# Where the third layer's weight sums are made, and when its first inputs are loaded

## The chip, the cores and the metric

The kernel runs on one core of a Trainium2 chip. The metric is the device time of one execution in microseconds (us); 1624.13 us is the median of three runs of the kernel before. The engines are named as in the profile: PE (TensorE; PEld is its weight load), DVE (VectorE), ACT (ScalarE), POOL (GpSimd) and SP (SyncE), whose queue issues the DMAs.

## What is computed

An attention over packed queries, followed by two feed-forward blocks. Everything is float32.

```python
def sm_attn(qq, kk, vv):                       # softmax attention, scale 1/8
    ...
p_packed = sm_attn(p, k, v)                    # 8 batches, 8 heads, 32 packed rows, 64 wide
x = sm_attn(q, p_packed, p_packed)             # 576 rows a batch -> 4608 tokens, 512 wide
h = x @ w_in;  x = (h * cos(h)) @ w_out        # first and second matrix, 512 x 2048, 2048 x 512
h = x @ w_in2; out = (h * tanh(softplus(h))) @ w_out2   # third and fourth matrix
```

## The kernel before

Each float32 factor of the big products is split into a high part (a cast, `hi`) and the rest (a subtraction, `lo`), and each product is three matmuls, high by high, high by low and low by high (lines 136 to 138).

The first part of the program is a loop of 256 steps, 16 tiles of 288 tokens by 16 blocks of 128 hidden columns. A step makes h of its block (the tile `ps`, one of four PSUM banks, lines 136 to 138 with `aT` and `wab`), the chain of cosine on ACT and DVE (L740, L742, L743, L749, L750), the split of the result (`gh`: L757 on ACT, L760 on POOL), and, three steps late, 12 matmuls of the second matrix into `acc`. After 16 steps the tile of outputs goes to DRAM (`evac`, L781, L783, through the tiles `xo` to `x2d`). L750 is the last instruction that reads a step's PSUM bank. Beside the steps a table of due times (`at_pe`, `at_ew`, `at_ld`) places work of other kinds: the attention of later batches, the first matrix's weights (`w_unit`, L496, L497), and `pre2`, which converts the third and fourth matrix from their input form (L413 and L415 load `raw`, L427, L428 and L432 convert, L437 stores to `ws` in DRAM). A scheduler then orders each engine's instructions; it does not keep to the order of the steps but lets an instruction go when its tiles are free, with higher priority for the chain.

The second part multiplies with the third matrix in seven products instead of eight (a Strassen scheme): tokens in five chunks of 1024, 1024, 1024, 1024 and 512, each cut into two halves, and hidden columns in eight blocks `p` of 256. For a block, seven weight combinations `k` are needed (four sums of quarters, three plain quarters), each split into hi and lo; for a chunk, seven input combinations (`X`, also four sums and three plain quarters). `product(i, p, k)` multiplies them in 6 matmuls, the results go through adds on DVE (L946), Mish on ACT (L957, L955) and a split (L898, L899), and `l4_subs` multiplies by the fourth matrix.

In the kernel before, `w2_comb(j)` makes the seven combinations of block j during the loop of steps, at steps 180, 187 and so on up to 229: two loads from `ws` (L525), four sums on DVE (L532 to L535), casts on ACT (L548), lo halves on POOL or DVE (L550), four stores to DRAM (`wst`, L553). The tiles are of the tags `ld`, `tmp` and `raw`, and `raw` (two buffers) is shared with the loads of `pre2`. The second part then loads each combination as a tile `ws` with a DMA of 256 KB (L877), five products ahead, for all five chunks.

The inputs of the first chunk come from `x2d`: `x_load` (L798) at steps 248 and 253, then `x_sums` (L810 to L813) and `x_split` (L824 on ACT, L825 on DVE or POOL) in the steps behind. The split tiles are of the tags `wa` and `wb` (`wab_tile`), four buffers each, which until steps 223 and 255 hold the first matrix's weights of the last two batches. The fourth matrix's weights are loaded and split by `w2o_load` (L566, L570, L574) from step 243 on.

Of the kernel before, what the change touches and what calls it, by code (L numbers as in the profile page):

```python
# [56 lines left out]
X2_AT = 248  # L57
COMB = (180, 7)
# [20 lines left out]
def build(tc, q, k, v, p, w1i, w1o, w2i, w2o, out):  # L79
    nc = tc.nc  # L80
    ctx = ExitStack()
    with ctx:
# [435 lines left out]
        def w2_comb(j):  # L518
            st = {}

            def load():
                st["c"] = []
                for c in range(2):
                    r = ld_tile([128, 512])
                    nc.sync.dma_start(r, w2s[("i", j, c)])  # L525
                    st["c"].append(r.rearrange("p (a f) -> p a f", f=256))

            def sums():
                c0, c1 = st["c"]
                a11, a21, a12, a22 = c0[:, :, :128], c0[:, :, 128:], c1[:, :, :128], c1[:, :, 128:]  # L530
                sa, sb = [tmp_tile([128, 2, 2, 128]) for _ in range(2)]
# [4 lines left out]
                st["b"] = ((a11, a12), (sa,), (sb,), (a22,))  # L536

            def split(k):
                def f():
                    parts = st["b"][k]  # L540
                    r = tp.tile([128, 2, 2, 2, 128], F32R, tag="raw", bufs=2, name=nm("hl"))
                    for x, src in enumerate(parts):
                        w = len(src.shape) == 4
                        for hl in range(2):
                            d = r[:, :, hl] if w else r[:, x, hl]
                            h = r[:, :, 0] if w else r[:, x, 0]
                            if hl == 0:
                                nc.scalar.copy(d, src)  # L548
                            else:
                                (nc.gpsimd if k < 2 else nc.vector).tensor_tensor(d, src, h, ALU.subtract)  # L550
# [3 lines left out]
                    for x in range(n):  # L554
                        WST[(j, ((0, 1), (5, 2), (6, 3), (4,))[k][x])] = t[:, x]
# [376 lines left out]
        for m in range(TMP_BUFS):  # L932
            ws_load(m)
# [106 lines left out]
```

## Time and profile before

| | |
|---|---|
| median of 3 runs | 1624.13 us (1622.72 to 1624.3) |
| the profiled execution's own time | 1623.2 us |
| its span, first to last instruction | 1621.4 us |
| granted clock of PE, mean | 0.983 |
| PE busy | 1533.1 us, 95% of the span |
| DVE, ACT, POOL busy | 961.3 us (59%), 813.2 (50%), 393.5 (24%) |

The loop of steps ends at about 882 us, and the second part takes the rest. The mean shares hide that the two parts differ: in the loop, DVE and ACT are busy for most of the time and PE has idle times; in the second part PE is busy throughout. So a stretch has to be read on its own, with PE's idle time and granted clock first, then who PE waits for, and then what that engine is doing.

### The profile page before, as it was taken

To read this page: it belongs to the slowest core of one execution; us is meant where nothing else is said; L and a number is where in the kernel's file an instruction comes from. 1 tells how busy PE (TensorE), PEld (TensorE's weight loads), DVE (VectorE), ACT (ScalarE), POOL (GpSimd) and SP (SyncE) were. 2 spreads that over 40 slices of the span, in tenths; PEclk is the share of its full clock that TensorE was granted. 3 is DMA by queue.
4 is the path that set the end of the run, shared out by engine and by line. 5 is a ranking of instruction groups with operands and counts; after the bars stand their busy time and mean duration, and the time that the engine had idled before them with its cause. 6 is when DMAs were issued, how large, how long until landed. Compare 5 with 4: busy or idle time off the path is not lost. (4 is left out here: it accounts for less than half of the span.)

```text
span 1621.4 us, 27105 instructions
## 1 busy us (share of the span) xinstructions
PE 1533.1 (95%) x9776; PEld 1292.4 (80%) x9776; DVE 961.3 (59%) x1894; ACT 813.2 (50%) x1640; POOL 393.5 (24%) x402
## 2 busy tenths in 40 slices
PE   3978999999999999988898999999999999999999
PEld 1557788799977998788796888888888888888898
DVE  4886667766756667787878436434643364435343
ACT  3665667665666666666665324323432343234233
POOL 0452323333323333444545002100110012001100
PEclk9789999999999999999999999999999999999999
DMA  9869685532635324655645333243424332433164
GB/s 289 280 193 219 163 217 153 132 90 66 174 88 146 90 69 151 236 175 203 219 153 168 127 124 124 75 143 121 128 72 143 124 120 67 141 122 123 53 197 135
DMA packets 143749, 235.61 MB, mean 145 GB/s; under 512 B 28928, under 2 KB 54016, under 8 KB 143616
## 3 DMA queue, kind: packets, MB, share of 16 engines
q1 hardware_dynamic: 143616, 233.89, 47.9%
q8 instruction: 77, 1.26, 0.3%
q14 instruction: 56, 0.46, 0.1%
HBM read 187.70 MB, written 46.14 MB: 144 GB/s over the span
## 5 line engine op out<-in xcount | busy, mean ns | idle before, releaser
L760 POOL TENSOR_TENSOR gh<-r,gh 128x288 fp32r<-128x288 f32 x256 | 215.5, 848 | 387.0 <-ACT gh L757 305.2
L137 PE MATMUL acc<-gh,wo 128*128 128x288 f32 x1024 | 303.7, 302 | 0.9 <-POOL gh L760 0.9
L138 PE MATMUL acc<-gh,wo 128*128 128x288 f32 x1024 | 298.3, 299 | 0.0
L136 PE MATMUL acc<-gh,wo 128*128 128x288 f32 x1024 | 284.4, 306 | 13.6 <-ACT gh L757 4.4
L136 PEld LDWEIGHTS acc<-gh,wo 128*128 128x128 f32 x1024 | 186.0, 192 | 49.7 <-issue 20.9
L137 PEld LDWEIGHTS acc<-gh,wo 128*128 128x128 f32 x1024 | 195.7, 191 | 15.2 <-issue 7.6
L138 PEld LDWEIGHTS acc<-gh,wo 128*128 128x128 f32 x1024 | 194.6, 191 | 6.6 <-issue 6.4
L136 PE MATMUL ps<-aT,wab 128*128 128x288 f32 x512 | 162.0, 316 | 21.8 <-DVE r L750 17.3
L749 ACT ACTIVATE r<-r,halfpi 128x288 f32<-128x288 f32 x256 | 136.0, 535 | 86.6 <-DVE r L743 81.9
L957 ACT ACTIVATE c<-c 128x512 f32<-128x512 f32 (+1 forms) x96 | 53.8, 561 | 242.6 <-DVE c L946 242.3
L740 ACT ACTIVATE ki<-ps,quarter 128x288 int32<-128x288 f32 x256 | 124.9, 495 | 61.6 <-PE ps L138 55.3
L137 PE MATMUL ps<-aT,wab 128*128 128x288 f32 x512 | 154.2, 301 | 0.0
L138 PE MATMUL ps<-aT,wab 128*128 128x288 f32 x512 | 153.7, 301 | 0.0
L750 DVE TENSOR_TENSOR r<-r,ps 128x288 f32<-128x288 f32 x256 | 114.6, 449 | 63.2 <-ACT r L749 62.2
L742 DVE SCALAR_TENSOR_TENSOR r<-ki,ps 128x288 f32<-128x288 int32 x256 | 114.0, 447 | 60.0 <-ACT ki L740 46.8
L136 PEld LDWEIGHTS ps<-aT,wab 128*128 128x128 f32 x512 | 98.9, 193 | 44.6 <-DVE r L750 23.7
L757 ACT CAST gh<-r 128x288 fp32r<-128x288 f32 x256 | 108.4, 429 | 50.1 <-DVE r L750 28.4
L743 DVE TENSOR_SCALAR r<-r 128x288 f32<-128x288 f32 x256 | 122.7, 482 | 3.8
L137 PE MATMUL acc<-wo,gh 128*128 128x512 f32 x320 | 125.0, 391 | 0.0
L136 PE MATMUL acc<-wo,gh 128*128 128x512 f32 x320 | 124.9, 390 | 0.0
L136 PE MATMUL ps<-wab,ws 128*128 128x512 f32 (+1 forms) x336 | 119.5, 356 | 5.1 <-DVE r L750 2.5
L138 PE MATMUL acc<-wo,gh 128*128 128x512 f32 x320 | 124.2, 389 | 0.0
(144 smaller groups left out, 3157.1 us busy)
## 6 DMA issues: line engine op xcount, KB each, us to landing
ws<-wst SPq DMA_DIRECT2D x280, 256.0 KB, 2.6
ld<-ws SPq DMA_DIRECT2D x96, 256.0 KB, 3.3
kr<-in_k_dram SPq DMA_DIRECT2D x64, 272.0 KB, 5.6
raw<-in_moe_w_out_dram SPq DMA_DIRECT2D x32, 512.0 KB, 4.4
kr<-in_q_dram SPq DMA_DIRECT2D x60, 272.0 KB, 5.5
wst<-hl SPq DMA_DIRECT2D x24, 512.0 KB, 3.1
x2d<-xo SPq DMA_DIRECT2D x64, 144.0 KB, 1.8
out_dram<-ld SPq DMA_DIRECT2D x36, 256.0 KB, 2.2
```

Source lines behind the costliest of these rows:

```text
L136: nc.tensor.matmul(ps, l0, r0, start=first, stop=False)
L137: nc.tensor.matmul(ps, l0, r1, start=False, stop=False)
L138: nc.tensor.matmul(ps, l1, r0, start=False, stop=last)
L740: nc.scalar.activation(ki, st["h"], AF.Identity, bias=quarter, scale=1.0 / TWO_PI)
L742: nc.vector.scalar_tensor_tensor(r, ki, -TWO_PI, st["h"], ALU.mult, ALU.add)
L743: (nc.gpsimd if n % C_MOD in C_POOL else nc.vector).tensor_scalar(r, r, 1.570796, -4.712388, ALU.min, ALU.max)
L749: nc.scalar.activation(g, g, AF.Sin, bias=halfpi, scale=1.0)
L750: nc.vector.tensor_tensor(g, g, st["h"], ALU.mult)
L757: nc.scalar.copy(gh[:, 0], st["g"])
L760: nc.gpsimd.tensor_tensor(gh[:, 1], st["g"], gh[:, 0], ALU.subtract)
L957: nc.scalar.activation(c, c, AF.Mish)
```

## The change

The sums and splits of the third matrix's weights leave the loop of steps, but for the first. `comb_load(0)` stands at step 240, `comb_sums(0)` at 242, the first five splits (`ws_load(0)` to `ws_load(4)`) at 243 to 247, `comb_load(1)` at 244. All others stand in the first chunk of tokens of the second part: after the first product of block p the sums of block p + 1 are made and the loads of block p + 2 issued, and after every product one more combination is split straight into the tile `ws` that a product five later uses, and stored to `wst`. The four later chunks load from `wst` as before. So for the first chunk 56 loads of 256 KB turn into 56 stores and 16 loads, and the loop of steps loses 16 loads and 32 stores less what blocks 0 and 1 need.

The inputs of the first chunk are loaded at steps 231 and 232 (into a `kr` tile, which the queries used), their sums stand at 233 and 234, four of the seven splits at 234 to 239 (into `wa`) and the other three at 247, 251 and 255 (into `wb`). One sum is now made in place. POOL makes the lo halves of the combinations with even k, DVE those with odd k; before it was the other way round. The last two also hold for the later chunks.

```diff
-X2_AT = 248
-COMB = (180, 7)
+X2_AT = 231
+COMB = 240
...
-        def w2_comb(j):
...
-                nc.vector.tensor_tensor(sa[:, 0], a21, a22, ALU.add)
-                nc.vector.tensor_tensor(sa[:, 1], sa[:, 0], a11, ALU.subtract)
-                nc.vector.tensor_tensor(sb[:, 1], a11, a21, ALU.subtract)
-                nc.vector.tensor_tensor(sb[:, 0], a12, sa[:, 1], ALU.subtract)
...
-                                (nc.gpsimd if k < 2 else nc.vector).tensor_tensor(d, src, h, ALU.subtract)
...
-                    nc.sync.dma_start(t, r[:, :n].bitcast(F32))
...
+        def comb_load(p):
+            CB[p] = []
+            for c in range(2):
+                r = ld_tile([128, 512])
+                nc.sync.dma_start(r, w2s[("i", p, c)])
+                CB[p].append(r.rearrange("p (a f) -> p a f", f=256))
+
+        def comb_sums(p):
...
+            r = tp.tile([128, 4, 2, 128], F32, tag="raw", bufs=2, name=nm("sw"))
+            nc.vector.tensor_tensor(r[:, 0], a21, a22, ALU.add)
+            nc.vector.tensor_tensor(r[:, 1], r[:, 0], a11, ALU.subtract)
+            nc.vector.tensor_tensor(r[:, 2], a11, a21, ALU.subtract)
+            nc.vector.tensor_tensor(r[:, 3], a12, r[:, 1], ALU.subtract)
+            CB[p] = (a11, a12, r[:, 1], r[:, 2], a22, r[:, 0], r[:, 3])
...
+        def ws_load(m):
...
+            w = WS[m] = tp.tile([128, 2, 2, 128], F32R, tag="tmp", bufs=TMP_BUFS, name=nm("ws"))
+            if m < 56:
+                nc.scalar.copy(w[:, 0], CB[p][k])
+                (nc.gpsimd if k % 3 == 2 else nc.vector).tensor_tensor(w[:, 1], CB[p][k], w[:, 0], ALU.subtract)
+                d = WST[(p, k)] = dram.tile([128, 2, 2, 128], F32, name=nm("wst"))
+                nc.sync.dma_start(d, w.bitcast(F32))
+            else:
+                nc.sync.dma_start(w.bitcast(F32), WST[(p, k)])
...
-        for j in range(8):
-            load, fs = w2_comb(j)
-            at_ld(COMB[0] + COMB[1] * j, load)
-            for i, f in enumerate(fs):
-                at_ew(COMB[0] + COMB[1] * j + 2 + i, f)
+        at_ld(COMB, lambda: comb_load(0))
+        at_ew(COMB + 2, lambda: comb_sums(0))
+        for m in range(TMP_BUFS):
+            at_ew(COMB + 3 + m, lambda m=m: ws_load(m))
+        at_ld(COMB + 4, lambda: comb_load(1))
...
+                if i == 0:
+                    r = kr_tile([128, 2, 1024])
+                    rs = [r[:, 0], r[:, 1]]
...
-                nc.vector.tensor_tensor(t1, b12, b11, ALU.subtract)
-                nc.vector.tensor_tensor(t2, b22, t1, ALU.subtract)
+                t2, t3, t4 = [ld_tile([128, 512])[:, :n] for _ in range(3)]
                 nc.vector.tensor_tensor(t3, b22, b12, ALU.subtract)
+                nc.vector.tensor_tensor(b12, b12, b11, ALU.subtract)
+                nc.vector.tensor_tensor(t2, b22, b12, ALU.subtract)
...
-                    X[(i, k)] = wab_tile(k // 4, [128, 2, 2, 512], F32R)
+                    X[(i, k)] = wab_tile((0, 1, 0, 0, 0, 1, 1)[k], [128, 2, 2, 512], F32R)
...
-                (nc.gpsimd if k % 2 else nc.vector).tensor_tensor(x[:, a, 1, :n], src, x[:, a, 0, :n], ALU.subtract)
+                (nc.gpsimd if k % 2 == 0 else nc.vector).tensor_tensor(x[:, a, 1, :n], src, x[:, a, 0, :n], ALU.subtract)
...
+        xu = x_units(0)
+        for a in range(2):
+            at_ld(X2_AT + a, xu[9 * a])
+            at_ew(X2_AT + 2 + a, xu[9 * a + 1])
+            for u, kk in enumerate((2, 3, 4, 0)):
+                at_ew(X2_AT + 3 + 2 * a + u, xu[9 * a + 2 + kk])
+            for u, kk in enumerate((1, 5, 6)):
+                at_ew(247 + 4 * u, xu[9 * a + 2 + kk])
...
             for a in range(2):
                 mm3(ps, w[:, 0, a], w[:, 1, a], x[:, a, 0, :n], x[:, a, 1, :n], a == 0, a == 1)
+            if i == 0 and k == 0 and p < 7:
+                comb_sums(p + 1)
+                if p < 6:
+                    comb_load(p + 2)
             ws_load(m + TMP_BUFS)
```

The change shifts the line numbers: L742, L743 and L750 of before are L734, L735 and L742 of the changed kernel, L784 is L776, L946 is L936 and L899 is L891.

DVE, among the steps at which the weights of the last pair of batches (`wab`, L497) are made. Before, the sums of the third matrix's first block (L532 to L535) stand between the chains:

```order
L532 TENSOR_TENSOR tmp_8483<-ld_8402,ld_8404 128x256
L534 TENSOR_TENSOR tmp_8484<-ld_8402 128x256
L533 TENSOR_TENSOR tmp_8483<-tmp_8483,ld_8402 128x256
L742 SCALAR_TENSOR_TENSOR r_8392<-ki_8390,ps_8369 128x288
L535 TENSOR_TENSOR tmp_8484<-ld_8404,tmp_8483 128x256
L743 TENSOR_SCALAR r_8392<-r_8392 128x288
L742 SCALAR_TENSOR_TENSOR r_8439<-ki_8437,ps_8406 128x288
L750 TENSOR_TENSOR r_8392<-r_8392,ps_8369 128x288
L743 TENSOR_SCALAR r_8439<-r_8439 128x288
L750 TENSOR_TENSOR r_8439<-r_8439,ps_8406 128x288
```

The changed kernel at the same weights, with its own line numbers (L804 and L805 are two sums of the inputs, in a `kr` tile):

```order
L734 SCALAR_TENSOR_TENSOR r_8517<-ki_8515,ps_8494 128x288
L735 TENSOR_SCALAR r_8517<-r_8517 128x288
L734 SCALAR_TENSOR_TENSOR r_8548<-ki_8546,ps_8525 128x288
L735 TENSOR_SCALAR r_8548<-r_8548 128x288
L742 TENSOR_TENSOR r_8517<-r_8517,ps_8494 128x288
L742 TENSOR_TENSOR r_8548<-r_8548,ps_8525 128x288
L734 SCALAR_TENSOR_TENSOR r_8589<-ki_8587,ps_8556 128x288
L735 TENSOR_SCALAR r_8589<-r_8589 128x288
L742 TENSOR_TENSOR r_8589<-r_8589,ps_8556 128x288
L804 TENSOR_TENSOR ld_10067<-kr_9986 128x512
L805 TENSOR_TENSOR kr_9986<-kr_9986 128x512
L734 SCALAR_TENSOR_TENSOR r_8629<-ki_8627,ps_8606 128x288
```

The four weight sums are gone from there, and the first sums of the inputs have come up from the end of the loop to this place.

SP, some forty steps on, where the fourth matrix is converted. Before (L553 stores a split of the third matrix's weights, L566 loads for the fourth matrix's splits):

```order
L553 DMA wst_9781<-hl_9778 128x1024
L437 DMA ws_9853<-tmp_9813 128x512
L553 DMA wst_9820<-hl_9817 128x512
L415 DMA raw_9822<-in_moe_w_out_dram 128x1024
L566 DMA ld_10697<-ws_9247 128x512
L415 DMA raw_9855<-in_moe_w_out_dram 128x1024
L415 DMA raw_9895<-in_moe_w_out_dram 128x1024
L437 DMA ws_9926<-tmp_9891 128x512
L437 DMA ws_9968<-tmp_9929 128x512
L566 DMA ld_10733<-ws_9295 128x512
L553 DMA wst_9980<-hl_9975 128x1024
L437 DMA ws_10011<-tmp_9971 128x512
```

The changed kernel, from the first of these raw loads on:

```order
L415 DMA raw_9053<-in_moe_w_out_dram 128x1024
L415 DMA raw_9055<-in_moe_w_out_dram 128x1024
L437 DMA ws_9086<-tmp_9049 128x512
L437 DMA ws_9124<-tmp_9089 128x512
L415 DMA raw_9093<-in_moe_w_out_dram 128x1024
L437 DMA ws_9167<-tmp_9127 128x512
L415 DMA raw_9136<-in_moe_w_out_dram 128x1024
L437 DMA ws_9169<-tmp_9132 128x512
L415 DMA raw_9176<-in_moe_w_out_dram 128x1024
L437 DMA ws_9207<-tmp_9172 128x512
L415 DMA raw_9565<-in_moe_w_out_dram 128x1024
L437 DMA ws_9248<-tmp_9210 128x512
```

The stores of hl and the loads of ld no longer stand between the raw loads and the stores of their conversions.

DVE in the third layer, from the first add of a block of weight columns on (c, u and m are the products' sums). Before:

```order
L946 TENSOR_TENSOR c_11692<-ps_11682,m_2264_11677 128x512
L946 TENSOR_TENSOR u_2271_11709<-ps_11700,m_2264_11677 128x512
L899 TENSOR_TENSOR gh_2267_11691<-c_11692,gh_2267_11691 128x512
L946 TENSOR_TENSOR u_2274_11723<-ps_11714,u_2271_11709 128x512
L946 TENSOR_TENSOR c_11738<-ps_11728,u_2274_11723 128x512
L946 TENSOR_TENSOR c_11755<-ps_11746,u_2274_11723 128x512
L946 TENSOR_TENSOR u_2271_11709<-ps_11746,u_2271_11709 128x512
L899 TENSOR_TENSOR gh_2277_11737<-c_11738,gh_2277_11737 128x512
L946 TENSOR_TENSOR c_11772<-ps_11763,u_2271_11709 128x512
```

The changed kernel, the second block (L531 to L534 are the sums of the next block, L547 a lo half):

```order
L936 TENSOR_TENSOR c_11307<-ps_11294,m_2148_11289 128x512
L547 TENSOR_TENSOR ws_11301<-sw_11131,ws_11301 128x256
L531 TENSOR_TENSOR sw_11419<-ld_11280,ld_11282 128x256
L533 TENSOR_TENSOR sw_11419<-ld_11280 128x256
L532 TENSOR_TENSOR sw_11419<-sw_11419,ld_11280 128x256
L936 TENSOR_TENSOR u_2157_11327<-ps_11315,m_2148_11289 128x512
L891 TENSOR_TENSOR gh_2152_11306<-c_11307,gh_2152_11306 128x512
L534 TENSOR_TENSOR sw_11419<-ld_11282,sw_11419 128x256
L547 TENSOR_TENSOR ws_11322<-ld_11136,ws_11322 128x256
L936 TENSOR_TENSOR u_2161_11344<-ps_11332,u_2157_11327 128x512
L547 TENSOR_TENSOR ws_11339<-ld_11138,ws_11339 128x256
L936 TENSOR_TENSOR c_11362<-ps_11349,u_2161_11344 128x512
```

Four sums and three lo halves now stand between the first five operations that this row had before; the row of a whole block has nine more.

## Rows read from the trace of the kernel before

**Rows 1.** Stretches of time: each engine's busy us and (x) instructions, granted clock, DMA share.

```profile
300.00:640.00 340.00, 335.81 (x2812) 294.34 (x2812) 230.24 (x541) 220.40 (x475) 121.99 (x139) 0.99 0.43 112
640.00:700.00 60.00, 56.35 (x432) 42.82 (x432) 46.43 (x94) 38.23 (x81) 27.11 (x28) 1.00 0.60 206
700.00:760.00 60.00, 50.05 (x346) 48.49 (x345) 47.45 (x103) 41.77 (x89) 27.19 (x29) 0.91 0.56 184
760.00:860.00 100.00, 91.42 (x668) 87.36 (x667) 79.83 (x161) 67.73 (x149) 48.88 (x52) 1.00 0.54 185
860.00:890.00 30.00, 22.10 (x112) 17.99 (x111) 24.22 (x31) 16.41 (x32) 15.43 (x12) 0.94 0.55 171
```

**Rows 2.** Waits of PE, 640 to 870 us: us in total, times, longest.

```profile
PE ps L136 <- DVE r L750: 15.6, 13, 4.2
```

**Rows 3.** DVE groups, 640 to 860 us: busy us, mean ns | idle before.

```profile
L743 DVE TENSOR_SCALAR r<-r 128x288 f32<-128x288 f32 x71 | 38.8, 547 | 0.7
...
L432 DVE SCALAR_TENSOR_TENSOR tmp<-tmp,cvt 128x512 int32<-128x512 int32 x17 | 13.2, 778 | 0.8 <-ACT tmp L427 0.3
...
L535 DVE TENSOR_TENSOR tmp<-ld,tmp 128x256 f32<-128x256 f32 x8 | 6.5, 811 | 0.0
L550 DVE TENSOR_TENSOR hl<-tmp,hl 128x512 fp32r<-128x512 f32 x8 | 5.8, 730 | 0.6 <-ACT hl L548 0.5
L534 DVE TENSOR_TENSOR tmp<-ld 128x256 f32<-128x256 f32 x8 | 5.5, 689 | 0.0
L550 DVE TENSOR_TENSOR hl<-ld,hl 128x256 fp32r<-128x256 f32 x8 | 4.5, 565 | 2.8 <-ACT hl L548 2.8
...
L532 DVE TENSOR_TENSOR tmp<-ld,ld 128x256 f32<-128x256 f32 x8 | 4.4, 546 | 0.8 <-DMA ld<-ws 0.7
```

**Rows 4.** The same view, 300 to 640 us: two groups.

```profile
L743 DVE TENSOR_SCALAR r<-r 128x288 f32<-128x288 f32 x114 | 50.6, 447 | 2.2
...
L432 DVE SCALAR_TENSOR_TENSOR tmp<-tmp,cvt 128x512 int32<-128x512 int32 x10 | 6.8, 684 | 0.0
```

**Rows 5.** Waits at the head of SP's queue, 640 to 860 us.

```profile
SPq L553 <- DVE hl L550: 27.7, 11, 4.5
SPq L553 <- POOL hl L550: 22.6, 11, 6.8
```

**Rows 6.** Groups of the whole span on POOL, DVE and ACT.

```profile
L825 DVE TENSOR_TENSOR wab<-ld,wab 128x512 fp32r<-128x512 f32 (+1 forms) x20 | 24.9, 1260 | 0.1
...
L550 POOL TENSOR_TENSOR hl<-ld,hl 128x256 fp32r<-128x256 f32 x16 | 12.2, 781 | 13.7 <-ACT hl L548 8.0 <-DMA raw<-in_moe_w_out_dram 5.7
...
L550 POOL TENSOR_TENSOR hl<-tmp,hl 128x512 fp32r<-128x512 f32 x8 | 11.2, 1404 | 4.8 <-ACT hl L548 4.6
...
L548 ACT CAST hl<-ld 128x256 fp32r<-128x256 f32 x24 | 9.2, 402 | 8.8 <-DMA wst<-hl 6.4 <-DMA ld<-ws 1.4 <-ACT gh L757 1.0
```

**Rows 7.** Stretches, as rows 1, in the third layer.

```profile
890.00:1004.00 114.00, 114.00 (x505) 94.39 (x504) 50.99 (x76) 37.83 (x62) 3.04 (x2) 1.00 0.39 127
1004.00:1046.00 42.00, 42.00 (x187) 34.77 (x186) 21.66 (x26) 15.18 (x27) 12.38 (x8) 1.00 0.24 70
```

**Rows 8.** Copies of m at L962, 870 to 1080 us: min/median/max ns, first to last start.

```profile
L962 ACT COPY m<-ps x8: 569/587/587, 883.1 to 981.4; 128x512 f32<-128x512 f32 x8
L962 ACT COPY m<-rb x3: 587/587/587, 1039.9 to 1069.8; 128x512 f32<-128x512 f32 x3
```

**Rows 9.** Three lines' instructions: min/median/max ns, first and last start.

```profile
L535 DVE TENSOR_TENSOR tmp<-ld,tmp x8: 410/630/1496, 644.3 to 796.0; 128x256 f32<-128x256 f32 x8
...
L550 DVE TENSOR_TENSOR hl<-ld,hl x8: 415/425/1014, 651.7 to 803.7; 128x256 fp32r<-128x256 f32 x8
...
L810 DVE TENSOR_TENSOR ld<-xr x10: 410/680/692, 845.6 to 1495.8; 128x512 f32<-128x512 f32 x8, 128x256 f32<-128x256 f32 x2
```

**Rows 10.** Timeline, 886 to 888 us: start, us, what [idle before].

```profile
886.10 0.46 DVE L783 COPY xo<-acc 128x288 f32<-128x288 f32 x1 [3.48 <-DMA x2d<-xo]
...
887.21 0.50 PE L136 MATMUL ps<-wab,ws 128*128 128x512 f32 x1 [1.86 <-DVE c L946]
```

More of the change, by code (lines that the diff above doesn't have):

```diff
@@ L516, in build @@
         WST = {}
-        def w2_comb(j):
[L519 to L531, printed above, removed]
-                nc.vector.tensor_tensor(sa[:, 0], a21, a22, ALU.add)
-                nc.vector.tensor_tensor(sa[:, 1], sa[:, 0], a11, ALU.subtract)
-                nc.vector.tensor_tensor(sb[:, 1], a11, a21, ALU.subtract)
-                nc.vector.tensor_tensor(sb[:, 0], a12, sa[:, 1], ALU.subtract)
[L536 to L549, printed above, removed]
-                                (nc.gpsimd if k < 2 else nc.vector).tensor_tensor(d, src, h, ALU.subtract)
-                    n = 1 if k == 3 else 2
-                    t = dram.tile([128, n, 2, 2, 128], F32, name=nm("wst"))
-                    nc.sync.dma_start(t, r[:, :n].bitcast(F32))
-                    for x in range(n):
-                        WST[(j, ((0, 1), (5, 2), (6, 3), (4,))[k][x])] = t[:, x]
-                return f
-            return load, [sums] + [split(k) for k in range(4)]
@@ new lines, in build @@
+        WS = {}
+        NQ = 56 * 5
+        def ws_load(m):
+            if m >= NQ:
+                return
+            p, k = divmod(m % 56, 7)
+            w = WS[m] = tp.tile([128, 2, 2, 128], F32R, tag="tmp", bufs=TMP_BUFS, name=nm("ws"))
[6 more added lines that the diff above has]
+                nc.sync.dma_start(w.bitcast(F32), WST[(p, k)])
@@ L791, in f @@
                 n = 1024 if i < 4 else 512
-                rs = []
-                for kc in (a, 2 + a):
-                    r = tp.tile([128, n], F32, tag="raw", bufs=2, name=nm("xr"))
+                if i == 0:
+                    r = kr_tile([128, 2, 1024])
+                    rs = [r[:, 0], r[:, 1]]
+                else:
+                    rs = [tp.tile([128, n], F32, tag="raw", bufs=2, name=nm("xr")) for _ in range(2)]
+                for r, kc in zip(rs, (a, 2 + a)):
                     lo, hi = 1024 * i, 1024 * i + n
@@ L808, in f @@
                 b11, b12, b21, b22 = b1[:, :n], b1[:, n:], b2[:, :n], b2[:, n:]
-                t1, t2, t3, t4 = [ld_tile([128, 512])[:, :n] for _ in range(4)]
-                nc.vector.tensor_tensor(t1, b12, b11, ALU.subtract)
-                nc.vector.tensor_tensor(t2, b22, t1, ALU.subtract)
+                t2, t3, t4 = [ld_tile([128, 512])[:, :n] for _ in range(3)]
                 nc.vector.tensor_tensor(t3, b22, b12, ALU.subtract)
+                nc.vector.tensor_tensor(b12, b12, b11, ALU.subtract)
+                nc.vector.tensor_tensor(t2, b22, b12, ALU.subtract)
                 nc.vector.tensor_tensor(t4, b21, t2, ALU.subtract)
-                raws[(i, a)] = (b11, b21, t2, t3, t4, t1, b22)
+                raws[(i, a)] = (b11, b21, t2, t3, t4, b12, b22)
             return f
@@ L860, in build @@
                 evac(m // NF)
-        for n in sorted(n for n in set(bg_pe) | set(bg_ew) | set(bg_ld) if n < X2_AT + 20):
+        for n in sorted(n for n in set(bg_pe) | set(bg_ew) | set(bg_ld)):
             run_bg(bg_pe, n)
@@ L930, in sub @@
                     todo.pop(0)()
-        for m in range(TMP_BUFS):
-            ws_load(m)
         for i in range(5):
```

16 lines of the change are left out of this document (3 added, 13 removed).

## The prediction

> **What bounds the kernel now.** I read first the busy time of the engines by stretch, then whom PE waited for, then the groups of DVE and the waits of SP in the stretch that stood out, and last the timeline at the change from the second matmul layer to the third.
>
> The stretches [rows 1] are to be read for two things: how long PE was idle, and whether its clock was whole. From 300 to 640 us PE is idle for 4.2 us and the granted clock is 0.99, worth 3.4 us more: 7.6 us of 340, or 2.2%. Later it is different: 3.65 us idle from 640 to 700, 9.95 from 700 to 760, 8.58 from 760 to 860, 7.90 from 860 to 890, together 30.1 us. In 700 to 760 us the granted clock is 0.91, which is 2.4 GHz with some time at 1.2 GHz in a stretch with much idle time, worth 0.09 x 60 = 5.4 us, and in 860 to 890 it is 0.94, 1.8 us. So 640 to 890 us loses 37 us; at 2.2% it would lose 5. The old sums of the third layer's weights sit just there: L535 runs from 644 to 796 us [rows 9]. After 890 us PE has no gap (114.00 of 114 us, 42.00 of 42) [rows 7]; nothing can be gained there.
>
> Whom PE waits for from 640 to 870 us: r at L750, which is DVE, 15.6 us in 13 waits [rows 2]. L750 is the last reader of the PSUM bank that holds a step's h, so DVE is late with the chain of a step and PE finds none of its four banks free. DVE is 77, 79, 80 and 81% busy in these stretches, 68% from 300 to 640 us [rows 1].
>
> **What goes from 640 to 860 us.** On DVE the old sums and lo halves are six groups: 6.5 + 5.8 + 5.5 + 4.5 + 4.4, and 4.4 again for L533, the twin of L532: 31.1 us [rows 3]. On POOL 12.2 + 11.2 = 23.4 us; on ACT 24 casts of 0.40 us and 16 of twice the width [rows 6]. On SP 16 loads and 32 stores. The stores stood at the head of SP's queue until their lo halves were made, 27.7 us for DVE and 22.6 us for POOL [rows 5], and behind them stood raw loads of the 17 conversions. In the new order of SP, raw loads and ws stores alternate with no hl store between.
>
> **What comes in.** Eight sums of the inputs and six of their lo halves (eight go to POOL) are DVE work of 0.68 to 1.26 us each [rows 9, 6], so 10 to 18 us. In the trace they begin at 846 us. In the new order the first sums stand among the very steps that lose the old ones, far ahead of step 231, since the scheduler lets work go once its tiles are free. The sums of two weight blocks and the first lo halves add some 12 operations of about 0.5 us, 6 us.
>
> **640 to 860 us, the sum.** Lost now: 22.2 idle + 5.4 clock = 27.6 us of 220, so the work itself is some 192 us. High end: if the loss of the quiet stretch goes with time, 2.2% of 192 = 4.2 us stay, a gain of 23.4. If that loss goes with its conversions, 17 against 10 [rows 3, 4], 1.7 x 7.6 = 13 us stay, a gain of 14.6. Low end: if the loss goes with DVE's work, only the net relief counts, 31.1 - 24 of 31.1, and the gain is 27.6 x 0.23 = 6.3. I take 14, near the middle of the three.
>
> **860 to 890 us.** Lost now: 7.9 + 1.8 = 9.7 us. The 1.86 us at the end [rows 10] stay: DVE's second evacuation waits 3.48 us for an xo store to land, and PE waits behind it; this isn't touched. The rest comes from the inputs' sums and lo halves and the fourth layer's weights falling together with the last steps. Most of the inputs' work has gone from here, but the new order has 91 second-layer matmuls in a row with no product between to fill a wait. Gain 0 to 7.8; I take 3.5.
>
> **The first 1024 tokens of the third layer.** A block of 256 weight columns takes 14.04 us: eight copies of m from 883.1 to 981.4 us are seven periods [rows 8]. DVE is 45% busy, 6.3 us a block; ACT 33%, 4.7 us [rows 7]. Added per block: on DVE four sums and five of seven lo halves (40 of 56), on ACT seven casts, on POOL two lo halves. A sum takes 0.41 us undisturbed, 0.81 in the mean of the dearest; a lo half 0.42 at least, 0.57 in the mean [rows 3, 9]. That is 3.7 to 6.1 us, so DVE comes to 10.0 to 12.4 of 14.04 us. ACT adds 7 x 0.40 = 2.8 and comes to 7.5. POOL gets 2 x 0.78. All fit, so PE's own 14.04 us hide the work. SP trades 56 loads of 256 KB for as many stores and 16 loads. Behind a late sum on DVE stand the adds that free PE's banks: a bank is wanted again four products later, 4 x 2.0 = 8 us after its product starts; the product takes 1.4 of them (6 matmuls of 114 / 505 = 0.226 us) and its add 0.7, so 6 us are slack. A weight tile is made five products ahead, with a similar margin. I charge 1 us for the first block, which stands without fourth-layer matmuls (42 x 0.226 = 9.5 us instead of 14); bounds 0 and 3.
>
> **Costed at nothing.** The in-place sum, three ld tiles instead of four and POOL making four of seven lo halves also hold for later tokens. The cover is the stage between the last block (981.4 + 14 us) and 1039.9 us [rows 8], 44 us in which PE works without a gap and the next inputs are split; without it one POOL lo half of 1.4 us would come late per chunk, some 6 us in four chunks.
>
> **The sum.** -14 - 3.5 + 1 = -16.5 us, against the profiled execution's own 1623.2 us (span 1621.4): 1606.7. The median of the runs is 0.9 us higher: 1607.5 us. With all ends the gain is 3 to 31 us, 1593 to 1621.
>
> **A rule weighed.** One sum took 0.41 to 1.50 us for the same shape [rows 9], and the chain's L743 took 547 ns from 640 to 860 us against 447 from 300 to 640 [rows 3, 4]. The Trainium skill, SBUF — State Buffer, section "Who interferes with whom", has a DVE tensor_tensor with two SBUF inputs contend with a GpSimd operation that reads SBUF: the second to issue blocks until the first is done; it lists tensor_scalar's faster modes as well. The trace agrees in kind: the longest sum is longer by 1.1 us, about one POOL operation. By the rule the POOL work that goes frees DVE of more than its own 31.1 us (the last rival), and the new sums in the third layer can each be blocked by a POOL lo half.
>
> **Rivals.**
> *DVE stays the bound.* 173.7 us of DVE from 640 to 860 us, less 31.1, plus 24, are 167 of some 206 us, 81%, no lighter than now. For it: the inputs land where DVE is already 77% busy. Against: the relief of SP and POOL. It gives the low end, 6.3 us, less 1: 1619 us. Chance 0.17.
> *The new work stalls the third layer; slower.* In each block four sums and lo halves stand nearly in a row on DVE between one product's add and the next. If PE waits out that row at mean prices, 0.55 + 0.69 + 0.55 + 0.81 + 2 x 0.57 = 3.7 us, eight blocks lose 30 us: 1637 us. It decides once such a row, with its wait for ACT's cast, exceeds the 6 us of slack, or once the nine added operations take more than 14.04 - 6.3 = 7.7 us a block, 0.86 us each. For it: maxima of 1.0 to 1.5 us [rows 9]. Against: POOL, next to which these maxima stood, is nearly idle in this stage (3.04 of 114 us) [rows 7]. Chance 0.09.
> *The whole hole closes.* DVE also gets back what POOL cost it, 71 x 0.10 = 7 us on L743 alone. Then 640 to 890 us runs at 2.2% and the 1.86 us: 37 - 5 - 2 = 30 us, 1594 us. Chance 0.07.
> My forecast has 0.67.
>
> **Range and chances.** A measurement of this kernel tells about 0.2%, 3.2 us, from no change. Faster: nearly all of the forecast, the last rival, more than half of the first: 0.82. Same: the rest of the first, and a stall in the third layer that eats the gain: 0.10. Slower: 0.08. The range for 8 in 10 is 1598 to 1620; it leaves out the second rival and most of the third.
>
> **What would show it.** Right: from 640 us to the first product PE loses some 13 to 20 us instead of 37, the clock is 1.00, waits for r at L750 are under 6 us, the first copy of m comes at about 866 us, and PE has no gap from then on with DVE at 70 to 88% for eight blocks. The step on the third layer is wrong if PE waits for a ws tile or for c and u in these blocks, or if a block takes over 14.3 us. The first step is wrong if L750 still leads PE's waits with more than 10 us.

## The result, and the profile of the changed kernel

The changed kernel takes 1597.52 us (median of 4 runs, 1596.92 to 1598.81) against 1623.43 us before (4 runs): a ratio of 0.9843, 95% interval 0.9826 to 0.986. The forecast was 1607.5 us, a gain of 16.5; the gain was 25.9. The time fell, as forecast, and it fell in the two places that were named; the size of one of the two was wrong, and the time lies 0.5 us below the range of 1598 to 1620.

The profiled execution took 1596.92 us (span 1595.1). Stretches, as in [rows 1] and [rows 7]; the last is the third layer's first 1024 tokens, which now begin 26 us earlier:

```profile
300.00:640.00 340.00, 334.87 (x2812) 293.67 (x2798) 227.84 (x540) 219.24 (x470) 119.95 (x136) 0.99 0.43 114
640.00:700.00 60.00, 59.60 (x464) 47.16 (x457) 40.50 (x88) 39.54 (x76) 19.61 (x21) 1.00 0.31 94
700.00:760.00 60.00, 52.34 (x376) 50.74 (x375) 51.84 (x106) 41.97 (x91) 30.54 (x30) 0.94 0.57 181
760.00:860.00 100.00, 95.16 (x694) 91.78 (x694) 76.10 (x154) 68.71 (x150) 50.97 (x51) 1.00 0.33 106
860.00:890.00 30.00, 30.00 (x134) 24.86 (x133) 20.99 (x44) 16.35 (x35) 4.45 (x5) 1.00 0.61 208
864.00:978.00 114.00, 114.00 (x504) 94.44 (x503) 67.29 (x130) 54.95 (x108) 12.58 (x15) 1.00 0.45 158
```

From 640 to 860 us PE is idle for 12.9 us, not 22.2, and from 860 to 890, where it is by now in the third layer, for none, not 7.9. What is left stands mostly from 700 to 760 us, where DVE is busier than before (51.84 against 47.45 us). All of PE's waits from 640 to 1020 us (total, times, longest), which answer to [rows 2]:

```profile
PE ps L136 <- DVE r L742: 11.7, 6, 4.7
PE acc L137 <- POOL gh L752: 0.6, 1, 0.6
PE acc L136 <- DVE xo L775: 0.4, 1, 0.4
```

Before, from 640 to 860 us, the three longest (xo is the evacuation of a tile: these waits are of the second matrix's matmuls for `acc`):

```profile
PE ps L136 <- DVE r L750: 14.5, 12, 4.2
PE acc L136 <- ACT xo L781: 3.5, 3, 2.3
PE acc L136 <- DVE xo L783: 1.6, 1, 1.6
```

So the waits for r fell by 2.8 us in this stretch, and those for xo by 4.7.

Copies of m in the third layer and the first one of the second 1024 tokens (rb), as in [rows 8], and two groups of DVE from 640 to 860 us, as in [rows 3]:

```profile
L952 ACT COPY m<-ps x8: 578/578/579, 857.5 to 955.4; 128x512 f32<-128x512 f32 x8
L952 ACT COPY m<-rb x5: 589/589/589, 1013.6 to 1073.4; 128x512 f32<-128x512 f32 x5
...
L735 DVE TENSOR_SCALAR r<-r 128x288 f32<-128x288 f32 x73 | 34.9, 481 | 1.0
...
L432 DVE SCALAR_TENSOR_TENSOR tmp<-tmp,cvt 128x512 int32<-128x512 int32 x17 | 15.5, 914 | 0.0
```

A block of weight columns takes (955.4 - 857.5) / 7 = 13.99 us, as before.

**Three marks cut the gain into parts.** ACT's first copy in the evacuation of a tile marks the tile's end; of the 16 tiles (0 to 15) I take the ends of tile 10 and tile 14. The third mark is the first rb copy. The middle part (M) from the first mark to the second is the old home of the weight sums; the end part (E) from the second to the third holds the last tile, the change of layers and all eight blocks of the first 1024 tokens, as many matmuls in every kernel here. Before, in the timeline of ACT (start, us):

```profile
630.04 0.70 ACT L781 COPY xo<-acc 128x288 f32<-128x288 f32 x2
837.16 0.69 ACT L781 COPY xo<-acc 128x288 f32<-128x288 f32 x2
```

and in the changed kernel:

```profile
627.64 0.69 ACT L773 COPY xo<-acc 128x288 f32<-128x288 f32 x2
821.36 0.39 ACT L773 COPY xo<-acc 128x288 f32<-128x288 f32 x1
```

With the rb copies at 1039.9 and 1013.6 us, M went from 207.1 to 193.7 us (13.4 less), E from 202.7 to 192.2 (10.5 less), and 2.4 us were gained ahead of 630 us, where the two programs have the same work. Together 26.3, the difference of the two profiled executions.

Between the first two marks, rounded to whole us, the engines were busy as follows, before and after:

```profile
630.00:837.00 207.00, 184.82 (x1353) 163.71 (x1350) 160.42 (x337) 136.43 (x294) 92.27 (x98) 0.98 0.58 198
```

```profile
628.00:821.00 193.00, 179.99 (x1349) 161.63 (x1342) 145.19 (x310) 127.91 (x269) 79.61 (x83) 0.98 0.37 120
```

PE's idle time went from 22.2 to 13.0 us, and the busy time of nearly the same number of matmuls from 184.8 to 180.0.

### The profile page after: what moved, and what is told of

Read it like the earlier page. It is cut to its first block, busy times and chain, and to the rows that moved or that the text cites. A ratio compares the mean times of both kernels' runs of the same rounds, so it can differ in the third digit from the quotient of the medians.

```text
span 1595.1 us, 27163 instructions
## 1 busy us (share of the span) xinstructions
PE 1523.9 (96%) x9776; PEld 1288.3 (81%) x9776; DVE 957.1 (60%) x1908; ACT 818.9 (51%) x1656; POOL 398.8 (25%) x404
## 5 line engine op out<-in xcount | busy, mean ns | idle before, releaser
L136 PE MATMUL ps<-aT,wab 128*128 128x288 f32 x512 | 160.9, 314 | 19.8 <-DVE r L742 14.6
L742 DVE TENSOR_TENSOR r<-r,ps 128x288 f32<-128x288 f32 x256 | 114.3, 449 | 63.9 <-ACT r L741 63.2
L734 DVE SCALAR_TENSOR_TENSOR r<-ki,ps 128x288 f32<-128x288 int32 x256 | 113.9, 447 | 62.7 <-ACT ki L732 50.1
L735 DVE TENSOR_SCALAR r<-r 128x288 f32<-128x288 f32 x256 | 116.4, 458 | 4.1
```

The source lines that it names most:

```text
L136: nc.tensor.matmul(ps, l0, r0, start=first, stop=False)
L734: nc.vector.scalar_tensor_tensor(r, ki, -TWO_PI, st["h"], ALU.mult, ALU.add)
L735: (nc.gpsimd if n % C_MOD in C_POOL else nc.vector).tensor_scalar(r, r, 1.570796, -4.712388, ALU.min, ALU.max)
L742: nc.vector.tensor_tensor(g, g, st["h"], ALU.mult)
```

## The experiments

Each kernel was timed in three rounds beside the kernel before. The column us is the median of the runs. M and E come from one profile each, and a profiled execution can lie off its median: that of e2 took 1618.88 us, 5.0 above, that of e1 1600.12, 3.5 below, those of e12 and e16 4.1 and 3.8 above. So differences of a few us in M are not told by these profiles alone.

| kernel | us | ratio, 95% interval | M | E |
|---|---|---|---|---|
| before | 1623.4 | 1 | 207.1 | 202.7 |
| e2, inputs alone | 1613.93 | 0.9927 to 0.9961 | 211.4 | 192.2 |
| e5, no sums | 1611.92 | 0.9908 to 0.995 | 196.2 | 202.4 |
| e6, no POOL lo halves | 1614.13 | 0.9909 to 0.996 | 195.4 | 204.1 |
| e7, no stores | 1612.99 | 0.9897 to 0.995 | 197.8 | 201.3 |
| e9, sums at 178 | 1613.83 | 0.9921 to 0.996 | 199.5 | 202.6 |
| e13, inputs at 247 | 1622.12 | 0.9971 to 1.0007 | 205.3 | 203.1 |
| e17, sums at 181 | 1620.18 | 0.996 to 0.9992 | 205.9 | 202.1 |
| e18, sums at 174 | 1620.85 | 0.9964 to 0.9993 | 205.8 | 201.9 |
| e14, conversions spread | 1619.91 | 0.9973 to 1.0 | 204.4 | 201.7 |
| e1, weights alone | 1603.66 | 0.9854 to 0.9896 | 187.9 | 201.5 |
| **changed** | 1597.52 | 0.9826 to 0.986 | 193.7 | 192.2 |
| e3, sums twice | 1596.57 | 0.981 to 0.9874 | 193.3 | 191.2 |
| e4, lo halves on POOL | 1598.14 | 0.9825 to 0.9869 | 192.8 | 191.2 |
| e8, first sums on POOL | 1599.57 | 0.9823 to 0.9866 | 192.7 | 192.2 |
| e16, weights at 238 | 1596.22 | 0.9815 to 0.986 | 192.1 | 192.4 |
| e10, inputs at 238 | 1594.67 | 0.9808 to 0.9848 | 188.0 | 193.3 |
| e12, conversions earlier | 1596.62 | 0.9816 to 0.9863 | 189.7 | 191.1 |
| e11, conversions spread | 1588.76 | 0.9765 to 0.9812 | 185.5 | 191.2 |
| e15, e10 and e11 | 1589.2 | 0.9773 to 0.9815 | 183.3 | 193.0 |

Rows down to e14 have the weight work of all eight blocks in the loop of steps, e5 to e7 less the part that is named; those from e1 on have little more there than the sums and first splits of the first two blocks.

### The two halves of the change, apart

e1 is the changed kernel with the inputs at their old steps, their splits in the old tiles and on the old engines (the load still goes to a `kr` tile, and one sum is in place); e2 is the kernel before with the inputs' part of the change alone.

```diff
-X2_AT = 231
+X2_AT = 248
...
-        xu = x_units(0)
...
+        for u, f in enumerate(x_units(0)):
```

> The weights' sums are made in the third layer as in the changed kernel, but the inputs of the first 1024 tokens stand at steps 248 and 253 as before, with the old engines and buffers for their splits (their load still goes to a kr tile and one sum is in place). Theory 1, two holes that add: the sums' removal fills 640 to 837 us (some 14 us) and the inputs' move fills the loop's end (some 10 us); this run then takes about 1609 us. Theory 2, the one on record: the inputs' move is worth 3.5 us at most; about 1601 us. Theory 3, the two need each other: 1609 us or more here, and no gain in the other run of this pair.

> The inputs are loaded and split as in the changed kernel (steps 231 and 232), while the weights' sums stay in the loop at steps 180 to 229 as before. Theory 1: about 1613 us. Theory 2: about 1620 us. Theory 3: the inputs' 10 to 18 us of DVE come into a stretch in which DVE is already late; 1622 us or more.

e1 gained 19.7 us, e2 9.4. No theory had e1's time; e2 came out by theory 1. The sum, 29.1 us, is more than the 25.9 of the whole change. The table tells where: the weights' part shortens M by 19.2 us and leaves E nearly as it was (201.5), the inputs' part shortens E by 10.5. In e2's profile M is 4.3 us longer, but not by waits:

```profile
632.00:843.00 211.00, 189.43 (x1340) 166.45 (x1333) 171.33 (x344) 140.08 (x299) 99.31 (x103) 0.94 0.60 204
```

PE's idle time is 21.6 us against 22.2 before; its busy time is 4.6 us longer, at a granted clock of 0.94 against 0.98. By the medians all of e2 but E lost only 1.1 us (10.5 - 9.4). That early inputs cost time in M is better seen between e1 and the changed kernel, where PE's waits for r in M are 5.7 and 11.7 us; M differs by 5.8, and by the medians the cost is 3.2 us (E's 9.3 less the 6.1 between the two times).

E's difference holds over all kernels: E is 201.3 to 204.1 us in the ten with late inputs and 191.1 to 193.3 in the ten with early ones, with nothing between. So the 10 us of E belong to the inputs' part, whatever else is done. This part moves the steps, the tiles of the splits and the engines of the lo halves together, and no run takes these three apart.

What stood in E is to be seen in PE's waits. Before, 837 to 890 us, the four longest:

```profile
PE ps L136 <- DVE r L750: 2.5, 2, 1.4
PE ps L137 <- DVE wab L825: 2.3, 1, 2.3
PE ps L136 <- DVE c L946: 1.9, 1, 1.9
PE ps L136 <- ACT m L962: 0.7, 1, 0.7
```

e1, 815 to 870 us, the three longest:

```profile
PE ps L136 <- DVE c L934: 2.5, 1, 2.5
PE ps L137 <- DVE wab L819: 2.3, 1, 2.3
PE ps L136 <- ACT m L950: 1.4, 1, 1.4
```

The wait of 2.3 us for wab is that of a third-layer product for its own input's lo half, which DVE had not made yet. DVE in the kernel before, at that time:

```profile
871.03 0.68 DVE L812 TENSOR_TENSOR ld<-xr,xr 128x512 f32<-128x512 f32 x1
871.63 0.44 DVE L750 TENSOR_TENSOR r<-r,ps 128x288 f32<-128x288 f32 x1
871.99 0.68 DVE L813 TENSOR_TENSOR ld<-xr,ld 128x512 f32<-128x512 f32 x1
872.60 1.78 DVE L825 TENSOR_TENSOR wab<-xr,wab 128x512 fp32r<-128x512 f32 x1
...
875.87 0.68 DVE L825 TENSOR_TENSOR wab<-ld,wab 128x512 fp32r<-128x512 f32 x1
```

The scheduler had let matmuls of the first third-layer products go ahead of the last tile's last matmuls, while their inputs were still being made; the first two of them, in PE's timeline, and the second-layer matmul behind them:

```profile
863.38 0.50 PE L136 MATMUL ps<-wab,ws 128*128 128x512 f32 x1 [1.15 <-DVE r L750]
863.72 0.40 PE L137 MATMUL ps<-wab,ws 128*128 128x512 f32 x1
863.95 0.30 PE L137 MATMUL acc<-gh,wo 128*128 128x288 f32 x1
```

L750 stood behind the sums, the product behind its lo half, and the next products behind the adds of c and u, which came after the evacuation on DVE. Which wait stands in the list differs: e13 and e18, with E as long (203.1 and 201.9 us), wait neither for wab nor for c, but for r:

```profile
PE ps L136 <- DVE r L750: 5.4, 4, 3.1
```

```profile
PE ps L136 <- DVE r L750: 5.7, 3, 4.1
```

What all ten kernels with late inputs share is that 21 to 24 product matmuls come before the last second-layer matmul; in the ten with early inputs none does. No run holds the products back while the inputs are late, so whether the early products or DVE's load at the end costs the 10 us stays open; only the inputs' part, which removes both, is shown.

In the changed kernel PE goes over without a gap (timeline of PE, start and us):

```profile
854.13 0.29 PE L138 MATMUL acc<-gh,wo 128*128 128x288 f32 x1
854.26 0.40 PE L136 MATMUL ps<-wab,ws 128*128 128x512 f32 x1
```

and the late second copy of the evacuation, with the adds of c and u behind it on DVE, is still there, but no product waits for them:

```profile
854.58 0.44 DVE L775 COPY xo<-acc 128x288 f32<-128x288 f32 x1
857.63 0.46 DVE L775 COPY xo<-acc 128x288 f32<-128x288 f32 x1 [2.61 <-ACT ws L546]
```

### Is the third layer near its limit?

e3 makes each of the sums of blocks 1 to 7 twice; e4 gives POOL all lo halves of the weights but the first five, which stay as they were.

```diff
-            nc.vector.tensor_tensor(r[:, 0], a21, a22, ALU.add)
+            for _ in range(2 if p else 1):
+                nc.vector.tensor_tensor(r[:, 0], a21, a22, ALU.add)
...
-                (nc.gpsimd if k % 3 == 2 else nc.vector).tensor_tensor(w[:, 1], CB[p][k], w[:, 0], ALU.subtract)
+                (nc.gpsimd if m >= TMP_BUFS or k % 3 == 2 else nc.vector).tensor_tensor(w[:, 1], CB[p][k], w[:, 0], ALU.subtract)
```

> The changed kernel, with the four sums of each block from the second on made twice (28 more DVE operations of 0.41 us or more, 1.6 to 2.6 us a block). If DVE has slack in the third layer, as the sum on record has it, nothing moves: 1597.5 us, blocks of 14.0 us. If the new work is close to stalling PE there, the blocks grow by up to 2.6 us, 18 us in all: 1605 to 1616 us.

> The changed kernel, with all 51 lo halves of the weights that are made in the third layer on POOL instead of 15. If POOL's reads block DVE's two-input operations as the longest rows of the kernel before suggest, 36 more POOL operations of 0.78 us cost DVE up to 28 us in the eight blocks, 3.5 us a block, and with DVE at about 11 us of 14 that is at the edge: 1597.5 to 1603 us. If PE's four banks and five weight tiles cover it: no change, 1597.5 us.

Neither moves the time. The stretch of the eight blocks, e3 first, then e4:

```profile
864.00:978.00 114.00, 114.00 (x505) 94.39 (x504) 76.99 (x153) 54.75 (x107) 13.86 (x16) 1.00 0.45 159
```

```profile
868.00:982.00 114.00, 114.00 (x505) 94.42 (x504) 58.94 (x96) 54.62 (x107) 37.87 (x48) 1.00 0.44 158
```

DVE at 68% with the sums made twice, or POOL three times as busy, leaves PE without a gap. The rival of a stalled third layer is out by a wide margin.

### What made the middle hole

e5, e6 and e7 each take one part of the old work out of the kernel before; e8 moves what is left of the sums in the loop to POOL.

```diff
-                nc.vector.tensor_tensor(sa[:, 0], a21, a22, ALU.add)
...
-                st["b"] = ((a11, a12), (sa,), (sb,), (a22,))
+                st["b"] = ((a11, a12), (a21, a22), (a12, a11), (a22,))
```

> The kernel before without the 32 DVE sums of the third layer's weights (L532 to L535, 20.8 us of DVE from 640 to 860 us in rows 3); quarters of the weights stand in their place, so the third layer multiplies by other numbers; casts, lo halves, loads and stores stay. Moving the weight sums alone gained 19.7 us (1603.7). Theory A, DVE's own busy time made the hole: 20.8 of 31.1 us of DVE go, so some 13 us of the 19.7: 1610 us, and e6 and e7 little. Theory B, the queues and POOL made it (SP's head waited 50.3 us for lo halves; a POOL operation holds DVE up): 3 to 5 us, 1618 to 1620 us.

```diff
+                        if k < 2:
+                            nc.scalar.copy(r[:, :, 0] if w else r[:, x, 0], src)
+                            continue
```

> The kernel before without POOL's 24 lo halves of the third layer's weights (L550 on POOL, 23.4 us of POOL); the hi half is stored once and loaded in both places. DVE's lo halves, the sums and the casts stay; the stores of these parts carry half the bytes and no longer wait for POOL (22.6 us at the head of SP's queue in rows 5). Theory A (DVE's own time): 1621 to 1623 us. Theory B (POOL's operations hold DVE up, and the stores that wait for them hold SP up): 8 to 12 us less, 1611 to 1615 us.

```diff
-                    nc.sync.dma_start(t, r[:, :n].bitcast(F32))
+                    if j == 0:
...
+                        nc.sync.dma_start(t, r[:, :n].bitcast(F32))
```

> The kernel before without 28 of the 32 stores of the third layer's weights (L553), those of blocks 1 to 7; the third layer reads block 0's weights in their place. All sums, casts and lo halves stay; gone are 7 MB of DMA and the waits of SP's queue for lo halves (50.3 us in rows 5), behind which the raw loads of the conversions stood. Theory A (DVE's own time): 1621 to 1623 us. Theory B (SP's queue): about 10 us less, 1611 to 1615 us.

```diff
+            eng = nc.gpsimd if p < 2 else nc.vector
+            eng.tensor_tensor(r[:, 0], a21, a22, ALU.add)
```

> The changed kernel with the eight sums of the first two blocks on POOL instead of DVE; they run at 794 to 805 us, where PE still waits 4.1 us for r. Theory A (DVE's own time is what PE waits for): DVE is freed of 5.6 us there and 2 to 3 of the 4.1 us go, 1594 to 1596 us. Theory B (a POOL operation holds DVE up for as long): no gain or a loss, 1597 to 1600 us.

The three gained 11.5, 9.3 and 10.5 us, 31 in sum, where the whole move gained 19.7. e5 came out near theory A (1610), e6 and e7 by theory B (1611 to 1615), so neither holds alone, and the parts don't add. e8 gave no gain that can be told (its interval overlaps the changed kernel's). e9 then put a question to these numbers: the same work, two steps earlier.

```diff
-COMB = (180, 7)
+COMB = (178, 7)
```

> The kernel before with the weight sums at steps 178, 185 and so on instead of 180, 187: the same work in nearly the same place. It asks how much a mere reshuffle of the order moves the time, since leaving out the sums, POOL's lo halves or the stores each gained 9 to 12 us. If those gains come from the work that was left out: within 3 us of the kernel before, 1620 to 1626 us. If the order of the kernel before is only an unlucky one: about 1612 us.

It gained 10.4 us against the kernel before of its own set (1624.25), without leaving anything out. The due times move the work by more than they say: the first block's sums begin at 619.6 us instead of 639.8, ahead of the first mark, and the last block's last sum at 775.7 instead of 796.0. Three more neighbours of the kernel before follow, e13 with `X2_AT = 247`, e17 with `COMB = (181, 7)`, e18 with `COMB = (174, 7)`, and one of the changed kernel, e16 with `COMB = 238`:

> The kernel before with the inputs' loads at step 247 and 252 instead of 248 and 253, a second neighbour that does the same work. If the order of the kernel before is an unlucky one, whose neighbours are all about 10 us faster: 1612 to 1616 us. If it was the move of the weight sums by two steps that gained in e9: 1621 to 1626 us.

> The kernel before with the weight sums one step later (181, 188 and so on). If the order of before is an unlucky one, a move to either side gains: 1612 to 1616 us. If earlier is better and later worse, because later sums meet the last conversions: 1624 to 1630 us.

> The kernel before with the weight sums six steps earlier (174, 181 and so on to 223). If earlier sums meet less of the conversions and the gain grows with the distance: 1600 to 1610 us. If the step of e9 was a lucky place: 1612 to 1626 us.

> The changed kernel with the loads, sums and first splits of the weights two steps earlier (COMB 238 instead of 240), a neighbour that does the same work, for the size of what a mere reshuffle does to the changed kernel. If the changed kernel's order is a typical one: 1595 to 1600 us. If it is a lucky one, as that of before looks unlucky: 1602 to 1608 us.

The neighbours of before lie at 1613.8, 1620.2, 1620.9 and 1622.1 us: no trend with the place (e17 is in neither of its ranges), 178 was a lucky one, and a mere reshuffle is worth from nothing that can be told (e13) to 10 us. The neighbour of the changed kernel is the same as it. Two things follow. The 9 to 12 us of e5 to e7 are hardly more than the luckiest of four reshuffles, so these runs can't share the hole out among DVE, POOL and SP; this stays open. And the change itself is outside the scatter: M is 199.5 to 211.4 us in the seven kernels that hold all the old weight work, 183.3 to 193.7 in the ten from which it was moved.

### What is left in the middle

e10 moves the inputs of the changed kernel to step 238; e11 spreads the conversions of the weights evenly, e12 spreads them from further ahead, e14 does e11 to the kernel before, e15 is e10 and e11 together.

```diff
-X2_AT = 231
+X2_AT = 238
```

> The changed kernel with the inputs' loads at steps 238 and 239, sums and first splits from 240 on instead of 233. If the gain at the loop's end needs only that the inputs' work is done before the last steps, and its early place costs the 6 us by which the changed kernel is slower in the middle than with the weights' part alone: 1593 to 1596 us. If the inputs' work is bound to collide with the last steps the later it comes: 1598 to 1602 us.

```diff
-PRE_AT = (43, 52, 49, 48, 53, 107, 108, 105, 106, 107, 171, 170, 171, 171, 172, 199, 203, 204, 205, 205, 206, 207, 208, 219, 221, 222, 223, 236, 237, 242, 241, 238)
+PRE_AT = (43, 52, 49, 48, 53, 107, 108, 105, 106, 107, 171, 170, 171, 171, 172, 180, 184, 188, 192, 196, 200, 204, 208, 212, 216, 220, 224, 228, 232, 236, 240, 241)
```

> The changed kernel with the 17 conversions of the fourth matrix's weights and the last of the third's spread evenly, one every four steps from 180 to 241, instead of in bursts from 199 to 208, 219 to 223 and 236 to 242. PE's waits for r that are left (11.7 us from 640 to 860) stand beside these conversions. If bursts of DVE work make them: 1588 to 1594 us. If only the sum of DVE's work counts: 1596 to 1600 us.

> The same conversions spread over steps 150 to 236, so that some eight of them move ahead of 640 us, where PE is idle for 4 us of 340. If DVE's work after 640 us makes the waits that are left: 1586 to 1592 us. If the waits follow the conversions to their new place: 1596 to 1600 us.

> The kernel before with the conversions spread evenly over steps 180 to 241 as in e11, the weight sums and inputs where they were. If the middle hole was DVE's, SP's and POOL's load as a whole, the sums keep it open and the spread gives no more than in the changed kernel (8.8 us): 1612 to 1620 us. If the bursts of conversions alone made it: 1600 to 1606 us, and then the change's move of the weight sums is only one of two ways to close it.

> The changed kernel with e10 and e11 together. If the two gains come from different waits they add: 1584 to 1587 us. If both take the same waits: 1588 to 1591 us.

e10's time, 1594.67 us, is in the first of its ranges, but it differs from that of the changed kernel by less than the intervals tell, and the edit hardly moved the work. The first sum of the inputs, in the changed kernel and in e10:

```profile
672.89 0.69 DVE L804 TENSOR_TENSOR ld<-kr 128x512 f32<-128x512 f32 x1
```

```profile
674.95 0.69 DVE L804 TENSOR_TENSOR ld<-kr 128x512 f32<-128x512 f32 x1
```

In both the scheduler lets these sums go far ahead of their steps; only the last two of the eight come later, by 27 and 37 us. So the 5.7 us by which its M is shorter can't be put down to a later place of the inputs. e11 takes 8.8 us more off the changed kernel, and its interval lies wholly below the changed kernel's: it is the best of all here, 1588.76 us. e15, the same spread with e10's inputs, has 1589.2, so the gain came twice; it is no better than e11, so the two gains don't add. e12's spread from step 150 gives nothing over the changed kernel: in its profile M is 4.0 us shorter, but from the end of tile 8 to that of tile 10, where conversions now stand, it takes 92.1 us instead of 89.6. e14's, while the sums stand beside the conversions, gives 3.6 us between the medians, with an interval that reaches to no change. Whether e11 gains by the even spacing or by one good order, these runs don't tell. Stretches of e11:

```profile
640.00:700.00 60.00, 58.40 (x470) 48.90 (x469) 47.85 (x98) 40.06 (x81) 21.33 (x23) 1.00 0.45 148
700.00:760.00 60.00, 55.69 (x414) 54.72 (x415) 46.76 (x102) 43.51 (x95) 32.45 (x33) 0.97 0.37 118
760.00:860.00 100.00, 96.55 (x678) 91.93 (x677) 77.72 (x158) 69.31 (x150) 48.18 (x48) 1.00 0.38 127
```

DVE's 700 to 760 us fell from 51.84 to 46.76 us and PE there went from 52.34 to 55.69; 640 to 700 us, which had room, took the work over.

## Why the prediction was right in kind and short by nine microseconds

**What bounds the kernel: right.** The loss stood from 640 to 890 us, PE waited for r, and nothing was to be gained from 890 us on.

**640 to 860 us, 14 taken: 13.4 measured by the marks**, which is partly luck. It is the net of two larger numbers, moving the weights alone (19.2 us off M) and the inputs' work that came in (5.8 us between e1 and the changed kernel, 3.2 by the medians), and the three ends near whose middle I took it (6.3, 14.6, 23.4) didn't part the two. The sign that I set for this step, waits for r at L750 under 6 us and the step wrong above 10, went against it: 11.7 us are left at L742. By my own sign the step's account of its waits was wrong. Of the 9.3 us of idle time that went from 640 to 860 us, 2.8 had that name (14.5 to 11.7); 4.7 were waits of second-layer matmuls for the evacuation xo (5.1 to 0.4), which the prediction doesn't name. The clock rose from 0.91 to 0.94 in 700 to 760 us, worth some 2 us, but not to the 1.00 that I had named. The sum of idle time and clock lost up to the first product, 16.5 us, is within the 13 to 20 that I had set.

**860 to 890 us, "I take 3.5": the step that failed.** E fell by 10.5 us, 0.4 of it in the eight blocks; the rest, 10.1, is the whole loss of 9.7 us that I had read there and a little more. Two sentences of that step were wrong. "The 1.86 us at the end stay": I took the wait behind the evacuation for a fixed cost of the evacuation. In the changed kernel DVE idles 2.61 us ahead of the same copy and PE has no wait, and in e13 and e18, with the inputs late and PE's list without c, the loss of E is as large. And the 91 second-layer matmuls in a row, which I feared, cost PE 0.6 us: with the inputs' work gone from DVE there was nothing to fill. That the wait was there because third-layer products had been let in early is the order seen in the traces, not a cause that a run isolates.

**The third layer, 1 us charged: nothing.** Blocks take 13.99 us instead of 14.04. The sums ran at their lowest price, 0.42 us, with POOL busy for only 12.58 of 114 us (in e4, with 37.87, two of the four sums took 0.52), and DVE stood at 59% (67.29 of 114 us), below the 70 to 88% that I had named.

**Costed at nothing, for later tokens: right.** From the first rb copy to the end of the span it is 1595.1 - 1013.6 = 581.5 us after, and 1621.4 - 1039.9 = 581.5 before.

**Ahead of 630 us: 2.4 us that aren't shown to be the change's.** Tile 10 ends at 626.4 to 634.1 us in the profiles of all kernels here but e12 (636.4), which moves conversions there on purpose (e9's and e18's first weight sums come before it too, and they lie inside, at 627.9 and 633.1). Kernels that differ from the changed one only in later steps (e3, e4, e8, e10, e16) span 627.0 to 634.1. Most of this scatter is older still: tile 2 ends at 241.9 us in the changed kernel, 245.4 before, and 241.9 to 249.1 in all. A single profile tells no more.

**The sum.** By the profiles the forecast of 16.5 us missed 9.8 of 26.3: 8.0 in E (10.5 against 3.5 less 1), 2.4 ahead of 630 us, and -0.6 in M.

**The rivals.** DVE staying the bound (1619) and a stalled third layer (1637) are out. The result lies between my forecast and "the whole hole closes" (1594), but not by that rival's reason: in the middle 12.9 us of idle time are left, and only the end closed. Of the 7 us that this rival gave back on the clamp, 4.8 came (547 to 481 ns, 73 times), while the conversions' L432 rose from 778 to 914 ns. The range was missed by 0.5 us, less than the 2.4 us ahead of 630; what was off by far more is the end step, whose bounds, 0 to 7.8, left out the 1.86 us as fixed.

**The rule weighed.** From 640 to 860 us, the clamp of the chain on DVE in the kernel before took 547 ns in the mean [rows 3]; in e6, without POOL's 24 lo halves, the same line:

```profile
L752 DVE TENSOR_SCALAR r<-r 128x288 f32<-128x288 f32 x72 | 30.3, 425 | 0.9
```

That is 0.122 x 72 = 8.8 us of DVE. The medians hardly differ (311 and 307 ns), so it is the number of long ones that fell. It isn't all POOL's: in e5, which keeps POOL's lo halves and drops DVE's sums, the mean is 488 ns:

```profile
L738 DVE TENSOR_SCALAR r<-r 128x288 f32<-128x288 f32 x73 | 35.4, 488 | 1.0
```

In e4, with POOL busy for 37.87 of 114 us, two groups of DVE (the add that reads PSUM, and the subtraction that reads SBUF twice):

```profile
L936 DVE TENSOR_TENSOR c<-ps,u 128x512 f32<-128x512 f32 x23 | 15.8, 690 | 15.0 <-PE ps L138 14.8
L891 DVE TENSOR_TENSOR gh<-c,gh 128x512 fp32r<-128x512 f32 x15 | 11.8, 786 | 0.2 <-ACT gh L890 0.2
```

In the changed kernel they take 686 and 682 ns:

```profile
L936 DVE TENSOR_TENSOR c<-ps,u 128x512 f32<-128x512 f32 x23 | 15.7, 686 | 12.7 <-PE ps L138 12.7
...
L891 DVE TENSOR_TENSOR gh<-c,gh 128x512 fp32r<-128x512 f32 x15 | 10.2, 682 | 0.2 <-ACT gh L890 0.2
```

So with more POOL work beside it the reader of two SBUF inputs became slower by 104 ns in the mean, and the reader of PSUM stayed as it was. The Trainium skill, SBUF — State Buffer, section "Who interferes with whom", has that a DVE instruction with two SBUF inputs contends with a GpSimd instruction that reads SBUF, and that one with at most one SBUF input and in no two-port mode doesn't. The trace of e4 agrees with this, but where DVE had room (e4) it cost PE nothing. The clamp reads SBUF once; the same section of the Trainium skill lists tensor_scalar among the operations that can enter a two-port mode, and whether this one did no run tells.

## What to carry to other kernels

Before a wait is put down as fixed, look at why its waiter was there at all: here PE stood behind an evacuation while later work had been let in ahead of its inputs, and with the inputs made early the wait was gone. When one part of a crowded stretch is left out and the time falls, run a neighbour that does the same work in a slightly other order before the gain is given to that part: three such parts "gained" 31 us of 20 here, and one lucky reshuffle gained about as much as any of them. A due time in a table isn't the time at which the work runs: look it up in the trace before a run is read. Marks that every kernel shares (a tile's end, the first copy of the next stage) part a gain into stretches better than the list of waits, as long as the profiled execution lies near its median.

## What the runs showed that I had not expected

A shift of a few entries of the table of due times, with the same work, moved the kernel before by up to 10 us (1613.8 to 1622.1 against 1623.4), though the medians of its own runs in the five sets lay between 1623.3 and 1624.3; I take it that a forecast of such a kernel from one trace can hardly be better than that. And an even spread of 17 conversions was worth 8.8 us in the changed kernel, and nothing that can be told in the one before.
